# Attention outputs made transposed, with probabilities divided before the product

## The chip, the cores and the metric

The kernel runs on one core of one Trainium2 chip. The metric is the device time of one execution in microseconds (us). A TensorE matmul holds one operand still in the array (the stationary one, loaded by LDWEIGHTS, up to 128 columns) and streams the other through it (the moving one). In the profile PE is the matmul side of TensorE, PEld its weight loads, DVE is VectorE, ACT ScalarE, POOL GpSimd, SP SyncE, which only issues DMAs here.

## What is computed

Eight batches of eight heads attend over 512 local tokens and 32 global ones, with head size 64. Then a mixture of eight experts, with weights from eight rounds of row and column division, runs over all 4352 tokens.

```python
s_g = scale * q_g @ concat(k_g, k_l).T          # 32 global queries see all 544 keys
out_g = softmax(s_g) @ concat(v_g, v_l)
s_ll = where(abs(i - j) <= 32, scale * q_l @ k_l.T, -1e9)
s_lg = scale * q_l @ k_g.T                      # local queries see a band and 32 global keys
out_l = softmax(concat(s_lg, s_ll)) @ concat(v_g, v_l)
x = attention outputs as (tokens, 512)
P = exp(x @ w_gate - max); 8 times: divide rows, divide columns, scale
out = sum over experts e of P[:, e] * (relu(x @ w1[e]) @ w2[e])
```

The experts' first product needs x with its 512 features on partitions: the persistent tile xT.

## The kernel before

**Units.** The attention stage goes through 32 units, one for each batch and head pair (index n, or s for the loop's turn). A unit's 512 queries are cut into eight blocks of 64. Block i sees a band of 128 keys and the 32 global keys, so its scores are 160 columns. The two heads of a pair lie on the two halves of the partitions, so one block is a tile of 128 rows (2 heads x 64 queries).

**Steps of a unit.** st_A transposes q and k on TensorE and spreads them (kTe, qbd). st_B, in three parts of three, three and two blocks, makes scores in PSUM (tile sc), lets VectorE apply the mask and find each row's extreme (ms, mx, L304) and lets ScalarE take the exponential (Pu, L307). st_D1 transposes the band part of the eight blocks on TensorE (ptw, L344) and VectorE copies it out (pw, L346). st_D2 does so for the global part: GpSimd gathers it (Pl, L341), TensorE transposes (L352), ScalarE copies (pg, L354). st_E, for the even blocks (par 0, values va) and the odd ones (par 1, values vb, shifted by 64 keys), multiplies: the transposed probabilities are stationary and V of the pair moves, 130 columns with a column of ones behind each head's 64 values. So the PSUM tile po has queries on its partitions, and the row sums stand in two of its columns. VectorE takes reciprocals (rr, L380) and multiplies them in on the way out (xn, L383). st_X transposes xn on TensorE (L361) and ScalarE copies it into xT (L362).

**Global groups.** Four heads' global queries of one batch form a group; there are 16. st_G0 spreads the queries on GpSimd (qgbd, L396), st_G1 makes 128x544 scores (sg, in po's PSUM buffer), VectorE takes the maximum (L408) and scales it (L409), ScalarE the exponential (Pg, L411). st_G2 transposes Pg in five pieces (L419, copied to pgs by ScalarE, L421). st_G3 multiplies by V (L431, L432) and divides on the way out, in turn on ScalarE (L444) and VectorE (L441), into xgn; st_G4 transposes xgn twice in all (L449, L451).

**Order.** Nothing is moved by a scheduler: each engine executes its instructions in the order in which the program text issues them. One turn s of the main loop runs: st_X(s-2), st_D1(s-1), two f1, st_B(s) part 0, st_D2(s-1), st_G2, st_B part 1, f2, st_E(s-1) par 0, st_A(s+1), f1, st_B part 2, st_E(s-1) par 1, st_G3, f2, logits (every fourth turn), f1 (from turn 9), st_G1, then DMAs and casts. st_G1 runs in turns 4 to 7 and then in every odd turn; st_G2 and st_G3 one turn later. The f1 and f2 are pieces of the experts 0 and 1 that fill TensorE: f1 is four matmuls (ph, L470) with a relu copy to hT on ScalarE or VectorE, f2 eight matmuls (py, L484) with a copy to yst (L487). Turns 0 to 3 have a loop of their own.

**Buffers in PSUM.** ps_mm has two (f1, f2), ps_sc two (scores, global outputs), ps_tr two (all transposes), ps_po one of two banks (po and sg). A buffer is written again only when its last reader is done.

After the stage come the routing weights (lines 842 to 913) and the experts 2 to 7 (lines 921 to 954), which the change does not touch.

Of the kernel before, what the change touches and what calls it, by code (L numbers as in the profile page):

```python
# [23 lines left out]
def kernel(  # L24
# [33 lines left out]
    VW = Dh + 1  # L58
# [30 lines left out]
    with tc.tile_pool(name="att_c", bufs=1) as att_c, \  # L89
# [17 lines left out]
        vgz = [att_c.tile([P, 4, H, VW], FP16, name=f"vgz{i}") for i in range(2)]  # L107
        qgbd = [att_c.tile([P, 2, P], FP16, name=f"qgbd{i}") for i in range(2)]
        vab = [(att_c.tile([P, NJ, H, VW], FP16, name=f"va{i}"),
                att_c.tile([P, NJ, H, VW], FP16, name=f"vb{i}")) for i in range(2)]  # L110
        xgn = [att_c.tile([P, D], FP16, name=f"xgn{i}") for i in range(2)]
# [35 lines left out]
        def select_v(b, t, js, both=True):  # L147
            for j in js:
                c0 = P * j + HB * t
                pv = ps_mm.tile([P, D], FP32, tag="mm", name="pv")  # L150
                for so in range(NJ):
                    nc.tensor.matmul(pv, zsel[:, so, c0 : c0 + P], vsr[:, so], start=(so == 0), stop=(so == NJ - 1))
                cp = nc.vector.tensor_copy if both and j % 2 == 0 else nc.scalar.copy
                cp(out=vab[b % 2][t][:, j, :, 0:Dh], in_=pv.rearrange("p (h d) -> p h d", h=H))
# [4 lines left out]
        def load_vz(b):  # L159
            for i in range(4):  # L160
                nc.sync.dma_start(out=vgz[b % 2][W * i : W * (i + 1), i, :, 0:Dh], in_=vg16[b])
# [7 lines left out]
        def load_v(b):  # L169
            va, vb = vab[b % 2]  # L170
            vz = vgz[b % 2]
            src = v_l[b].rearrange("h s d -> s h d")

            def first():
                load_vg(b)
                nc.gpsimd.dma_start(out=va[W:P, 0, :, 0:Dh], in_=src[0:96])

            def mid(j):
                nc.gpsimd.dma_start(out=va[:, j, :, 0:Dh], in_=src[P * j - W : P * j + 96])

            def last():
                nc.gpsimd.dma_start(out=vb[HB : HB + W, NJ - 1, :, 0:Dh], in_=src[Sl - W : Sl])
                move_vb(b)
                load_vz(b)

            return [first] + [lambda j=j: mid(j) for j in range(1, NJ)] + [last]
# [25 lines left out]
        def init_vgz(t, eng):  # L212
            eng.memset(t, 0.0)
            for i in range(4):
                eng.memset(t[W * i : W * (i + 1), i, :, Dh:VW], 1.0)

# [23 lines left out]
        for va, vb in vab:  # L240
            nc.vector.memset(va[:, :, :, Dh:VW], 1.0)
            nc.vector.memset(vb[:, :, :, Dh:VW], 1.0)
# [41 lines left out]
        def st_B(n, part):  # L284
            b, hp = divmod(n, HP)
            qb, kt = qbd[n % 2], kTe[n % NK]
            if part == 0:
                st[n] = dict(Pu=att_wk.tile([P, NHB, SW], FP16, tag="Pu", name="Pu"),
                             mx=att_wk.tile([P, NHB], FP32, tag="mx", name="mx"))
            d = st[n]  # L290
            i0 = 3 * part
            ni = min(3, NHB - i0)
            sc = ps_sc.tile([P, 512], FP32, tag="sc")
            ms = att_wk.tile([P, 3, SW], FP32, tag="ms")
            for ii in range(ni):
                i = i0 + ii
                nc.tensor.matmul(sc[:, SW * ii : SW * ii + KW], qb[:, i, :],  # L297
                                 kt[:, HB * i : HB * i + KW], start=True, stop=True)
                nc.tensor.matmul(sc[:, SW * ii + KW : SW * (ii + 1)], qb[:, i, :],  # L299
                                 kgT[:, hp, Sg * b : Sg * (b + 1)], start=True, stop=True)  # L300
            for ii in range(ni):
                i = i0 + ii
                mi = 0 if i == 0 else (2 if i == NHB - 1 else 1)
                nc.vector.tensor_tensor_reduce(  # L304
                    out=ms[:, ii, :], in0=sc[:, SW * ii : SW * (ii + 1)], in1=mask[:, mi, :],
                    scale=-scale, scalar=BIG, op0=ALU.add, op1=ALU.min, accum_out=d["mx"][:, i : i + 1])
                nc.scalar.activation(out=d["Pu"][:, i, :], in_=ms[:, ii, :], func=AF.Exp, scale=-1.0,  # L307
                                     bias=d["mx"][:, i : i + 1])

        def st_B0(n, part):  # L310
            b, hp = divmod(n, HP)
            qb, kt = qbd[n % 2], kTe[n % NK]
            if part == 0:
                st[n] = dict(Pu=att_wk.tile([P, NHB, SW], FP16, tag="Pu", name="Pu"),
                             mx=att_wk.tile([P, NHB], FP32, tag="mx", name="mx"))
# [17 lines left out]
            for ii in range(ni):  # L333
                i = i0 + ii
                nc.scalar.activation(out=d["Pu"][:, i, :], in_=sc[:, SW * ii : SW * (ii + 1)], func=AF.Exp,
                                     scale=-1.0, bias=d["mx"][:, i : i + 1])

        def st_D1(n):
            d = st[n]
            d["Pl"] = att_wk.tile([P, NHB, Sg], FP16, tag="Pl", name="Pl")  # L340
            nc.gpsimd.tensor_copy(out=d["Pl"], in_=d["Pu"][:, :, KW:SW])  # L341
# [14 lines left out]
        def st_X(n):  # L356
            b, hp = divmod(n, HP)
            xn = st.pop(n)["xn"]
            pt = ps_tr.tile([P, NJ, P], FP16, tag="tr")
            for j in range(NJ):  # L360
                nc.tensor.transpose(pt[:, j, :], xn[:, j, :], identity)  # L361
            nc.scalar.copy(out=xT[:, hp, Sl * b : Sl * (b + 1)], in_=pt.rearrange("p j q -> p (j q)"))  # L362

        def st_E(n, par):
            b, hp = divmod(n, HP)
            d = st[n]
            va, vb = vab[b % 2]
            vz = vgz[b % 2]
            if par == 0:
                d["xn"] = att_wk.tile([P, NJ, P], FP16, tag="xn", name="xn")  # L370
            vx = va if par == 0 else vb
            po = ps_po.tile([P, NJ, 256], FP32, tag="po")
            for j in range(NJ):
                i = 2 * j + par
                nc.tensor.matmul(po[:, j, 0 : 2 * VW], d["pw"][:, i, :], vx[:, j, 2 * hp : 2 * hp + 2, :],  # L375
                                 start=True, stop=False)
                nc.tensor.matmul(po[:, j, 0 : 2 * VW], d["pg"][:, i // 4, :], vz[:, i % 4, 2 * hp : 2 * hp + 2, :],  # L377
                                 start=False, stop=True)
            rr = att_wk.tile([P, NJ], FP32, tag="rr")
            nc.vector.reciprocal(out=rr, in_=po[:, :, Dh])  # L380
            for a in range(2):
                r = slice(HB * a, HB * (a + 1))
                nc.vector.tensor_tensor(out=d["xn"][HB * par : HB * (par + 1), :, Dh * a : Dh * (a + 1)],  # L383
                                        in0=po[r, :, VW * a : VW * a + Dh],
                                        in1=rr[r].unsqueeze(2).to_broadcast([HB, NJ, Dh]), op=ALU.mult)
# [12 lines left out]
        def st_G1(b, g):  # L398
# [8 lines left out]
            m2 = att_wk.tile([P, 2], FP32, tag="m2")  # L407
# [3 lines left out]
            nc.scalar.activation(out=Pg, in_=sg[:, 0:S], func=AF.Exp, scale=scale, bias=m2[:, 1:2])  # L411
            gs[(b, g)] = Pg

        def st_G2(b, g):
            Pg = gs[(b, g)]
# [8 lines left out]
        def st_G3(b, g):  # L424
# [3 lines left out]
            po = ps_sc.tile([P, 512], FP32, tag="sc")  # L428
            hs = slice(4 * g, 4 * g + 4)
            for t in range(NJ):  # L430
                nc.tensor.matmul(po[:, 0 : 4 * VW], pgs[:, t, :], vb[:, t, hs, :], start=(t == 0), stop=False)  # L431
            nc.tensor.matmul(po[:, 0 : 4 * VW], pgs[:, 4, :], vz[:, 3, hs, :], start=False, stop=True)  # L432
            rg = att_wk.tile([P, 1], FP32, tag="rg")
            nc.vector.reciprocal(out=rg, in_=po[:, Dh : Dh + 1])
            xg = xgn[b // 4]
            o = slice(W * (b % 4), W * (b % 4 + 1))
            for hh in range(4):
                r = slice(W * hh, W * (hh + 1))
                h = 4 * g + hh
                if hh % 2:  # L440
                    nc.vector.tensor_scalar(out=xg[o, Dh * h : Dh * (h + 1)], in0=po[r, VW * hh : VW * hh + Dh],  # L441
                                            scalar1=rg[r, 0:1], scalar2=None, op0=ALU.mult)
                else:
                    nc.scalar.mul(xg[o, Dh * h : Dh * (h + 1)], po[r, VW * hh : VW * hh + Dh], rg[r, 0:1])  # L444

        def st_G4(hf):
            pt = ps_tr.tile([P, HP, P], FP16, tag="tr")
            for dk in range(DP):
                nc.tensor.transpose(pt[:, dk, :], xgn[hf][:, P * dk : P * (dk + 1)], identity)  # L449
            t0 = (GT0 + hf) * P  # L450
            nc.scalar.copy(out=xT[:, :, t0 : t0 + P], in_=pt)  # L451
# [99 lines left out]
        for s in range(HP):  # L551
# [5 lines left out]
            if s >= 2:  # L557
                st_X(s - 2)
# [24 lines left out]
            st_A(s + 1)  # L583
            if s == 1:
# [16 lines left out]
        for s in range(HP, NU + 2):  # L601
# [8 lines left out]
            if s == HP:  # L610
                st_D1(s - 1)
                st_D2(s - 1)
                st_X(s - 2)
# [4 lines left out]
                st_X(s - 1)  # L618
# [8 lines left out]
            else:  # L627
                if s > HP + 1:
                    st_X(s - 2)
                if s > NU:  # L630
                    break
# [11 lines left out]
            if s < NU:  # L643
                st_B(s, 1)
            f2("a")
# [5 lines left out]
            if s < NU:  # L651
                st_B(s, 2)
            if s > HP:
# [9 lines left out]
            if s == 17:  # L663
                st_G4(0)
            if s == NU:
                st_G4(1)
# [319 lines left out]
```

## Time and profile before

| | us |
|---|---|
| three runs: lowest, median, highest | 1085.76, 1086.7, 1090.41 |
| the profiled execution: its time | 1088.94 |
| its span, first to last instruction | 1087.2 |
| attention stage, last copy into xT ends | about 359 |

Busy times inside the attention stage, of 50 us from 200 to 250: PE 49.44, DVE 35.44, ACT 37.09, POOL 13.43. The granted TensorE clock is 1.00 there and 0.991 over the span.

| group | engine | count | mean ns |
|---|---|---|---|
| L307 exponential, 128x160 | ACT | 224 | 422 |
| L304 mask and extreme, 128x160, and its read of the result | DVE | 224 | 321 and 83 |
| L380 reciprocal 128x4 | DVE | 64 | 180 |
| L383 division on the way out, 64x256 | DVE | 128 | 422 |
| L361 transposes of outputs | PE | 128 | 221 |
| L362 copy into xT, 128x512 | ACT | 32 | 585 |
| L341 gather Pl, 128x256 | POOL | 32 | 400 |
| L129 casts of q and k, 128x1024 | POOL | 30 | 1046 |

Matmuls are pipelined: one row lasts longer than the step to the next. So TensorE's cost is read from the starts of neighbours, not from the mean. A line of the timeline gives start, length, engine, line, operation and, in brackets, how long the engine had stood idle before it and what ended that.

### The profile page before, as it was taken

To read this page: it belongs to the slowest core of one execution; us is meant where nothing else is said; L and a number is where in the kernel's file an instruction comes from. 1 tells how busy PE (TensorE), PEld (TensorE's weight loads), DVE (VectorE), ACT (ScalarE), POOL (GpSimd) and SP (SyncE) were. 2 spreads that over 40 slices of the span, in tenths; PEclk is the share of its full clock that TensorE was granted. 3 is DMA by queue.
4 is the path that set the end of the run, shared out by engine and by line. 5 is a ranking of instruction groups with operands and counts; after the bars stand their busy time and mean duration, and the time that the engine had idled before them with its cause. 6 is when DMAs were issued, how large, how long until landed. Compare 5 with 4: busy or idle time off the path is not lost.

```text
span 1087.2 us, 19737 instructions
## 1 busy us (share of the span) xinstructions
PE 1050.2 (97%) x7988; PEld 685.3 (63%) x7988; DVE 697.7 (64%) x1504; ACT 540.2 (50%) x1091; POOL 126.6 (12%) x232
## 2 busy tenths in 40 slices
PE   7689999999999999999999999999999999999987
PEld 4555665666665455666666666666666666666676
DVE  6667676767676666768457466576575474485474
ACT  5658777777766445334334334343343343343332
POOL 7251332231401500000000000000000000000000
PEclk8989999999999999999999999999999999999999
DMA  9956676785753977423423424524424334234242
GB/s 257 195 99 168 101 170 184 114 181 145 136 103 66 215 172 289 184 97 137 174 98 136 175 97 141 185 87 175 179 99 173 137 136 175 97 136 144 104 169 79
DMA packets 102963, 160.55 MB, mean 148 GB/s; under 512 B 40909, under 2 KB 75865, under 8 KB 91865
## 3 DMA queue, kind: packets, MB, share of 16 engines
q1 hardware_dynamic: 52376, 120.03, 32.4%
q0 software_dynamic: 46736, 20.20, 15.3%
q10 hardware_dynamic: 3760, 19.08, 4.5%
q8 instruction: 62, 1.02, 0.4%
q14 instruction: 29, 0.23, 0.1%
HBM read 149.24 MB, written 33.40 MB: 168 GB/s over the span
## 4 chain that ended last, share of the span: by engine, by line
PE 81%; DVE 9%; DMA 3%; ACT 2%; issue 2%; SPq 1%; POOL 0%; DVEq 0%; ACTq 0%; POOLq 0%
PE ph L772 32%; PE m L808 20%; PE pm L808 8%; PE ph L470 8%; PE py L484 7%; DVE xn L383 3%; DMA qgf<-in_q_g_dram 1%; DVE hT L475 1%; PE sc L297 1%; PE po L377 1%; DVE ms L304 1%; PE po L375 1%; DMA pb<-pd 1%; SPq L192 1%; ACT yst L487 1%
## 5 line engine op out<-in xcount | busy, mean ns | idle before, releaser
L774 ACT ACTIVATE h<-ph 128x512 f16<-128x512 f32 (+1 forms) x432 | 247.1, 573 | 397.7 <-PE ph L772 393.8
L772 PE MATMUL ph<-xs,w1s 128*128 128x512 f16 (+1 forms) x1728 | 405.3, 367 | 3.6 <-DMA w1s<-w1d 2.3
L772 PEld LDWEIGHTS <-w1s 128*128 128x128 f16 x1728 | 169.0, 98 | 128.3 <-issue 2.6
L814 DVE SCALAR_TENSOR_TENSOR o<-pm,o 128x512 f32<-128x512 f32 (+1 forms) x106 | 70.6, 667 | 241.3 <-PE pm L808 241.0
L808 PEld LDWEIGHTS <-h 128*128 128x128 f16 x1616 | 158.1, 98 | 48.4
L808 PE MATMUL m<-w2c,s 128*128 128x256 f16 x1212 | 158.3, 273 | 0.0
L808 PEld LDWEIGHTS <-s 128*128 128x128 f16 x1212 | 118.6, 98 | 43.8
L470 PE MATMUL ph<-xT,w1e 128*128 128x512 f16 (+1 forms) x576 | 135.2, 368 | 3.7 <-DVE lg L459 1.4
L484 PE MATMUL py<-w2e,hT 128*128 128x512 f16 x544 | 128.3, 379 | 0.1
L708 DVE TENSOR_TENSOR xs<-xT,pb 128x2048 f16<-128x2048 f16 (+2 forms) x57 | 117.2, 2060 | 11.1 <-DMA pb<-pd 11.1
L808 PE MATMUL m<-w2c,h 128*128 128x256 f16 x808 | 105.5, 273 | 0.0
L808 PE MATMUL pm<-w2c,h 128*128 128x256 f16 x808 | 96.9, 273 | 0.0
L708 DVE TENSOR_TENSOR s<-h 128x2048 f16<-128x2048 f16 (+1 forms) x106 | 92.3, 912 | 4.5 <-ACT h L774 4.5
L470 PEld LDWEIGHTS <-w1e 128*128 128x128 f16 x576 | 54.6, 99 | 51.5 <-issue 6.8
L484 PEld LDWEIGHTS <-hT 128*128 128x128 f16 x544 | 50.8, 97 | 51.0 <-issue 0.2
L307 ACT ACTIVATE Pu<-ms,mx 128x160 f16<-128x160 f32 x224 | 80.8, 422 | 3.2 <-DVE mx L304 1.7
L304 DVE CUSTOM_DVE_ANT_0 ms<-sc,mask 128x160 f32<-128x160 f32 x224 | 59.7, 321 | 34.6 <-PE sc L299 17.9
L708 DVE TENSOR_TENSOR h<-h 128x1024 f16<-128x1024 f16 (+1 forms) x106 | 65.6, 660 | 0.0
L383 DVE TENSOR_TENSOR xn<-po,rr 64x256 f16<-64x256 f32 x128 | 54.0, 422 | 3.1
L473 ACT ACTIVATE hT<-ph 128x512 f16<-128x512 f32 (+1 forms) x91 | 48.9, 564 | 13.8 <-PE ph L470 11.4
L814 DVE SCALAR_TENSOR_TENSOR o<-m,o 128x512 f32<-128x512 f32 (+1 forms) x90 | 52.2, 653 | 0.4
L487 ACT COPY yst<-py 128x512 f32<-128x512 f32 x68 | 39.5, 581 | 21.0 <-PE py L484 18.7
(156 smaller groups left out, 971.1 us busy)
## 6 DMA issues: line engine op xcount, KB each, us to landing
w1s<-w1d SPq DMA_DIRECT2D x54, 1024.0 KB
yd<-yst ACTq DMA_DIRECT2D x16, 1024.0 KB
pb<-pd SPq DMA_DIRECT2D x48, 256.0 KB
o<-yd SPq DMA_DIRECT2D x8, 1024.0 KB
y<-yd SPq DMA_DIRECT2D x8, 1024.0 KB
out_dram<-o SPq DMA_DIRECT2D x8, 1024.0 KB
f<-in_q_l_dram SPq DMA_DIRECT2D x15, 512.0 KB
f<-in_k_l_dram SPq DMA_DIRECT2D x15, 512.0 KB
```

Source lines behind the costliest of these rows:

```text
L304: nc.vector.tensor_tensor_reduce(out=ms[:, ii, :], in0=sc[:, SW * ii : SW * (ii + 1)], in1=mask[:, mi, :], scale=-scale, scalar=BIG, op0=A ...
L307: nc.scalar.activation(out=d["Pu"][:, i, :], in_=ms[:, ii, :], func=AF.Exp, scale=-1.0, bias=d["mx"][:, i : i + 1])
L383: nc.vector.tensor_tensor(out=d["xn"][HB * par : HB * (par + 1), :, Dh * a : Dh * (a + 1)], in0=po[r, :, VW * a : VW * a + Dh], in1=rr[r]. ...
L470: nc.tensor.matmul(ph[:, 0:n], wts[e][0][:, dk, P * fm : P * (fm + 1)], xT[:, dk, c0 : c0 + n], start=(dk == 0), stop=(dk == DP - 1))
L473: nc.scalar.activation(out=hT[:, fm, 0:n], in_=ph[:, 0:n], func=AF.Relu)
L484: nc.tensor.matmul(py, hT[:, fk, P * c : P * (c + 1)], wts[e][1][:, fk, :], start=(fk == 0), stop=(fk == FT - 1))
L487: nc.scalar.copy(out=ys[:, c, :], in_=py)
L708: nc.vector.tensor_tensor(out=out, in0=in0, in1=in1, op=op)
L772: nc.tensor.matmul(ph[:, 0:n], w1s[i][:, dk, P * fm : P * (fm + 1)], xss[i][:, dk, 0:n], start=(dk == 0), stop=(dk == DP - 1))
L774: nc.scalar.activation(out=hs[i][:, fm, 0:n], in_=ph[:, 0:n], func=AF.Relu)
L808: nc.tensor.matmul(pm[:, HD * t : HD * (t + 1)], lhs[0][:, k, lhs[1] + P * t : lhs[1] + P * (t + 1)], w[:, q - 1, k, :], start=(k == 0 and ...
L814: nc.vector.scalar_tensor_tensor(out=o, in0=pm[:, 0 : HD * nt].rearrange("p (t d) -> p t d", d=HD), scalar=sg / float(E), in1=o, op0=ALU.m ...
```

## The change

V of the pair becomes the stationary operand and the transposed probabilities move. The product then comes out with the pair's 128 features on partitions and 64 queries of each head side by side, as xT wants it; of each 128x128 block the two 64x64 diagonal parts are used. The sums come from the exponentials themselves (accum_out), and a new step st_N divides the probabilities before they are transposed: a reciprocal for each part and a multiply for each block on VectorE, and one multiply with a broadcast for the global part on GpSimd, which now makes Pl. st_X and st_G4 go, with the ones columns (130 columns become 128, and vgz lands in rows of 1024 bytes instead of 128). For global groups st_GN divides Pg, ahead of st_D1 in the text.

```diff
-                                     bias=d["mx"][:, i : i + 1])
+                                     bias=d["mx"][:, i : i + 1], accum_out=d["sm"][:, i : i + 1])
...
+        def st_N(n, part):
...
+            nc.vector.reciprocal(out=d["rs"][:, i0:i1], in_=d["sm"][:, i0:i1])
+            for i in range(i0, i1):
+                nc.vector.tensor_scalar(out=d["Pu"][:, i, 0:KW], in0=d["Pu"][:, i, 0:KW], scalar1=d["rs"][:, i : i + 1],
+                                        scalar2=None, op0=ALU.mult)
+            if part == 2:
...
+                nc.gpsimd.tensor_tensor(out=d["Pl"], in0=d["Pu"][:, :, KW:SW],
+                                        in1=d["rs"].unsqueeze(2).to_broadcast([P, NHB, Sg]), op=ALU.mult)
...
-            d["Pl"] = att_wk.tile([P, NHB, Sg], FP16, tag="Pl", name="Pl")
-            nc.gpsimd.tensor_copy(out=d["Pl"], in_=d["Pu"][:, :, KW:SW])
...
+                nc.tensor.matmul(po[:, i, :], vx[:, j, 2 * hp : 2 * hp + 2, :], d["pw"][:, i, :], start=True, stop=False)
+                nc.tensor.matmul(po[:, i, :], vz[:, i % 4, 2 * hp : 2 * hp + 2, :], d["pg"][:, i // 4, :],
                                  start=False, stop=True)
...
+            if par == 1:
+                for a, cp in ((0, nc.scalar.copy), (1, nc.vector.tensor_copy)):
+                    r = slice(HB * a, HB * (a + 1))
+                    cp(out=xT[r, hp, Sl * b : Sl * (b + 1)].rearrange("p (i q) -> p i q", q=HB), in_=po[r, :, r])
...
+        def st_GN(b, g):
+            Pg, m2 = gs[(b, g)]
+            nc.vector.reciprocal(out=m2[:, 3:4], in_=m2[:, 2:3])
+            nc.vector.tensor_scalar(out=Pg, in0=Pg, scalar1=m2[:, 3:4], scalar2=None, op0=ALU.mult)
...
+            for pr in range(2):
+                hs = slice(4 * g + 2 * pr, 4 * g + 2 * pr + 2)
+                qs = slice(HB * pr, HB * (pr + 1))
+                for t in range(NJ):
+                    nc.tensor.matmul(po[:, pr, :], vb[:, t, hs, :], pgs[:, t, qs], start=(t == 0), stop=False)
+                nc.tensor.matmul(po[:, pr, :], vz[:, 3, hs, :], pgs[:, 4, qs], start=False, stop=True)
...
+                cp(out=xT[r, 2 * g : 2 * g + 2, t0 : t0 + Sg], in_=po[r, :, Sg * a : Sg * (a + 1)])
```

The calls in a turn of the main loop:

```diff
             else:
-                if s > HP + 1:
-                    st_X(s - 2)
-                if s > NU:
-                    break
+                if g23:
+                    st_GN(*gp)
                 st_D1(s - 1)
...
                 st_B(s, 1)
+                st_N(s, 0)
...
                 st_B(s, 2)
+                st_N(s, 1)
             if s > HP:
                 st_E(s - 1, 1)
...
             f2("a")
-            if s == 17:
-                st_G4(0)
-            if s == NU:
-                st_G4(1)
+            if s < NU:
+                st_N(s, 2)
```

In turns 0 to 3 the three parts of st_N stand together behind st_A(s+1).

## Prediction

> **What bounds the kernel now.** I read the page's busy times first, then its slices, then a table of stretches, the chain of waits, and the timelines of single engines over two units.
>
> ```profile
> PE 1050.2 (97%) x7988; PEld 685.3 (63%) x7988; DVE 697.7 (64%) x1504; ACT 540.2 (50%) x1091; POOL 126.6 (12%) x232
> ```
>
> TensorE is busy nearly all the time. The change touches the attention stage alone, which ends near 359 us, so that stage is what counts:
>
> ```profile
> core 0: us, PE busy (x) PEld busy (x) DVE busy (x) ACT busy (x) POOL busy (x), PEclk, DMA share, GB/s
> 200.00:250.00 50.00, 49.44 (x463) 31.00 (x461) 35.44 (x140) 37.09 (x87) 13.43 (x25) 1.00 0.66 134
> ```
>
> In a stretch of 50 us TensorE idles 0.56. VectorE works 71% of it and ScalarE 74%: both have room on the average. What counts is whether each of their results is there when TensorE, which takes its instructions in order, comes to need it. The chain of waits gives the period of two units (a unit is one head pair; every second one carries a global group):
>
> ```profile
> 198.18 1.73 PE ph L470 x8
> ...
> 219.20 1.73 PE ph L470 x8
> ```
>
> So a pair of units lasts 21.02 us. TensorE's own steps, added from the starts in its timeline, make 20.64; 0.38 is waiting.
>
> Now ScalarE over one unit that carries a global group:
>
> ```profile
> 219.67 0.71 ACT L411 ACTIVATE Pg<-sg,m 128x544 f16<-128x544 f32 x1 [1.74 <-DVE m L409]
> 220.28 0.57 ACT L362 COPY xT<-pt 128x512 f16<-128x512 f16 x1
> 220.75 1.10 ACT L473 ACTIVATE hT<-ph 128x512 f16<-128x512 f32 x2
> 221.74 1.07 ACT L307 ACTIVATE Pu<-ms,mx 128x160 f16<-128x160 f32 x3
> 222.71 0.35 ACT L354 COPY pg<-pt 128x256 f16<-128x256 f16 x1
> 222.96 0.69 ACT L421 COPY pgs<-pt 128x640 f16<-128x640 f16 x1
> 223.55 1.07 ACT L307 ACTIVATE Pu<-ms,mx 128x160 f16<-128x160 f32 x3
> 224.51 0.57 ACT L487 COPY yst<-py 128x512 f32<-128x512 f32 x1
> 225.85 1.17 ACT L282 COPY qbd<-pt 64x512 f16<-64x512 f16 x2 [0.77 <-DVE kTe L273]
> 227.05 0.75 ACT L307 ACTIVATE Pu<-ms,mx 128x160 f16<-128x160 f32 x2
> ```
>
> The reader is to see that from 219.67 to 227.80 it stands still once, for 0.77 us. And two engines that read one score tile take turns, though their partitions differ:
>
> ```profile
> 207.23 0.30 ACT L444 ACTIVATE xgn<-po,rg 32x64 f16<-32x64 f32 x1 [0.45 <-DVE rg L434]
> 207.57 0.28 DVE L441 TENSOR_SCALAR xgn<-po,rg 32x64 f16<-32x64 f32 x1 [0.37 <-ACT xgn L444]
> ```
>
> **The change part by part.** TensorE first. Four transposes of outputs go from each unit: four of L361 take 0.22 us in a row (starts 0.055 apart). The global product goes from five matmuls of 260 columns (0.54 us, starts 0.11 apart) to ten of 64. No row has 64 columns with a new weight: the 32-column score matmuls and the 8-column logits matmuls both step by 0.027 us, the 128-column ones by 0.055. I take 0.027, thus 0.27 us (at 0.055 nothing is won). The pair product goes from 130 to 128 columns, 0.8 ns each. A pair of units saves 2 x 0.22 + 0.27 + 32 x 0.0008 = 0.74 us. The two groups of L449 go as well (0.44 us in all).
>
> ScalarE: the exponentials give sums. Whether this costs an instruction the trace does not show. VectorE's counterpart does: DVE_READ_ACCUMULATOR2, 83 ns, 224 times. Ends: nothing, and 202 ns (L244, an ACTIVATE of one column). I take 0.083, the same job on the neighbour; eight a unit make 0.66 us. The copy L362 (0.585) is replaced by a copy of 64x512 (0.58, as L282).
>
> VectorE: per unit two L380 and four L383 go, 2.05 us. Three reciprocals (0.18, as L380), eight divides of 128x128 and one copy of 64x512 (0.69, as L154) come. A divide between SBUF tiles of f16 has no row. Ends: 0.154 (L409, one column) and 0.287 (L848, 128x128 to f32); I take 0.21, as the f16 copy L548 of that shape. Sum 0.54 + 1.68 + 0.69 = 2.91. Each global group loses 0.74 (L434, two L441) and gains a reciprocal 0.17, a divide of 128x544 (ends 0.154 and 0.72, one column and one element a cycle; taken 0.44, at L346's pace) and a copy 0.22. VectorE goes from 7.4 to about 8.3 us per unit of 10.5, ScalarE from 7.8 to about 8.3. Neither is full. The loss is in the order:
>
> A. The divide of the global probabilities (st_GN) stands on VectorE ahead of the copy pw, and the global transposes on TensorE need both: Pg divided, and the PSUM buffer that pw frees. Count from the end of the global scores (218.37). In the profile the exponential ends at 220.38, 2.01 later. Add the sum's read 0.08, reciprocal 0.17, divide 0.44, pw 0.68 and four hand-overs of 0.04 (rr to xn): 3.54. TensorE is there after ptw 0.45, two ph 1.73, scores 0.24 and two transposes 0.11: 2.53. It waits 1.0; with VectorE later by 0.4 from the unit before (step C), 1.4. Before, pw ran while the exponential did.
>
> B. The unit's last divides (part 2) stand on VectorE behind its copy of the outputs, which waits for ScalarE's copy of the same tile (the turn-taking above), which stands behind the last exponentials. First exponential at 3.54 + 0.4 + 0.37 (L304's 0.32 and a hand-over) = 4.3. ScalarE then needs 2.77 (221.74 to 224.51), yst 0.57, qbd 1.17, exponentials 0.75, eight reads 0.66, copy 0.58: done at 10.8. Then VectorE's copy 0.69, the global copy 0.22, reciprocal 0.18, two divides 0.42, hand-overs 0.16: 12.5. TensorE, late by A, comes to the seventh probability transpose of the next unit at 2.53 + 1.4 + 7.46 + 0.33 = 11.7 (7.46 are its steps from the global transposes on). It waits 0.8. Before, these transposes needed only exponentials, long done.
>
> C. In the other unit the same queue holds the copies of the outputs until 10.5; the next global scores need that buffer and come at 10.3: 0.1 to 0.2, and VectorE's backlog pushes A by 0.4. The copy pg also slips behind its first matmul: 0.1.
>
> New waits 1.4 + 0.8 + 0.1 + 0.1 = 2.4 a pair; saved work 0.74; of the old waits some 0.3 (L470 behind yst L487 and behind lg L459) go under the new ones. Net +1.35 a pair. Units 9 to 32 make 12 pairs: +16.2. In units 5 to 8 each carries a group and there is one f1 less before the scores: waits of about 1.9, less 0.49 of work and 0.5 of old waits, +0.9 each: +3.6. At the start TensorE idles until q_g has landed (53.5 us); the change saves nothing there, and Pl, now behind the divides, holds back GpSimd's casts and the loads on SP's queue behind them by up to 1.1 us, with the DMA engines full anyway: +0.5. vgz lands in longer rows (32 KB each as now), behind q_g in its queue: nothing. At the end the two last output transposes with their waits (0.62 and 0.24) go: -1. Sum +19.3. The profiled execution took 1088.94 (span 1087.2), so it would take 1108.2; on the median, 1086.7 + 19.3 = 1106.0.
>
> A rule against the waits in B: the Trainium skill, PSUM — Partial Sum Buffer, section on bank collisions, has two engines collide only in the same bank and quadrant, so the halves of po could be copied side by side. The trace differs in what is done: all 32 of L441 wait for ScalarE. Were the rule used, B and C would shrink by 0.69 us and the sum by some 8 us.
>
> **Rivals.** 1. TensorE stays the bound and the change is faster. Place: the global transposes (A) and the seventh transpose (B). It holds if the new waits of a pair stay under 0.74 + 0.3 = 1.04 us. For it: VectorE and ScalarE are only 71 and 74% busy, and TensorE loses real work. Against it: A alone is 1.0 with no delay from elsewhere. With no wait at all: 12 x -1.04, 4 x -0.5, -1: -15.5, 1071 us. Chance 0.10.
>
> 2. The costs taken are at their low ends: the sum comes free, the divide of Pg takes 0.15. Then B falls to 0.14, C to nothing, A to about 1.1: +0.2 a pair, with start, end and units 5 to 8 about +3 in all: 1090. For it: ScalarE has free time in the other units. Chance 0.16.
>
> 3. The divides wait for GpSimd. They are the first VectorE operations of the stage that both read and write SBUF alone, and GpSimd is busy 13.43 of 50 us with casts of 1.046. If the two exclude each other, each of some 3.5 groups of divides a unit meets a busy GpSimd with chance 0.27 and waits half a cast: 0.47 a unit, over 28 units +13 on the forecast: 1119; with the sum's read at its high end of 0.2 (B and C each 0.9 more) up to 1145. The trace of before has no such pair of operations in this stage. The Trainium skill, SBUF — State Buffer, Who interferes with whom, states this exclusion for tensor_scalar in its two-port modes; no run here shows it yet. Chance 0.14.
>
> **How the numbers follow.** The forecast of 1106 has 0.60, with its own range of 1092 to 1128. The bounds of the read (0 to 0.2) and of the divides carry it from 1087 to 1145; the range that leaves out most of rival 1 and the far end of rival 3 is 1084 to 1138. Under about 0.5% (5.4 us) this kernel's measurement does not tell a change from none. Faster by more: rival 1, 0.10. Within: rival 2 with a little of the forecast's edge, 0.16. Slower: 0.74.
>
> **What would show it.** Right: L419's successor waits for DVE pw, over 0.8 us each; the ptw transposes wait for VectorE's divide; VectorE's xT copy waits for ScalarE's; TensorE in 200 to 250 us falls from 49.44 to about 44.5 busy; the pair of units lasts 22.4 us. Wrong: TensorE still near 49 there (rival 1); no row for reading sums on ScalarE (rival 2); divides whose times scatter by up to a cast (rival 3). It goes wrong above all if the read costs far from 0.083, as eight stand in each chain.

## The result, and the profile after

The changed kernel takes 1118.3 us (median of four runs, 1117.4 to 1122.7) against 1086.2 for the kernel before in the same session (1084.7 to 1090.4): ratio 1.030, 95% interval 1.026 to 1.034, so it is slower by 32 us. The profiled execution has a span of 1120.9 us and took 1122.7, the longest of the four; the other three lie at 1117.4 to 1118.8. Most of that difference seems to lie in its first 60 us, as will be seen.

First the page's busy times and the stretch from 200 to 250 us, the same views as of before:

```profile
PE 1053.5 (94%) x7932; PEld 679.6 (61%) x7932; DVE 734.7 (66%) x1692; ACT 555.2 (50%) x1345; POOL 132.6 (12%) x224
```

```profile
200.00:250.00 50.00, 44.63 (x412) 26.96 (x413) 37.73 (x157) 36.24 (x115) 13.25 (x23) 1.00 0.64 139
```

TensorE's busy time in that stretch falls from 49.44 to 44.63 us, at the full granted clock both times, while VectorE is 75% and ScalarE 72% busy. No engine is full over the stretch, so the time goes into waits between them. The chain of waits of the changed kernel shows the hand-overs (start, duration, what ran):

```profile
210.24 1.73 PE ph L459 x8
...
217.27 0.93 ACT Pu L301 x4
218.23 0.59 ACT xT L380
218.84 0.69 DVE xT L380
219.57 0.18 DVE rs L339
219.77 0.80 DVE Pu L341 x2
...
221.39 0.64 DVE m L404
...
222.30 0.81 ACT Pg L407 x2
...
223.34 0.36 DVE Pg L414
223.70 0.60 DVE pw L354
...
224.63 1.34 ACT Pu L301 x6
...
226.82 1.25 ACT Pu L301 x6
...
233.41 1.74 PE ph L459 x8
```

This pair of units lasts 23.17 us; the same pair took 22.00 before (186.84 to 208.84). Pairs differ in length: the one of 21.02 us that the prediction shows lasts 22.69 now, and the mean of the ten pairs from unit 10 to unit 30 (counted from 0) goes from 21.45 to 23.12. From 217.27 to 233.19 us TensorE is not in the chain at all. First come the last exponentials with their sums (4 entries: two exponentials, two reads), ScalarE's copy of the outputs, VectorE's copy of the same tile, the reciprocal, the last divides and the maximum of the next global scores. Then the global exponential on ScalarE at 222.30, the divide of the global probabilities, and only then the copy pw that sets TensorE free. From there ScalarE runs on through the next unit's exponentials and reads, the copies pgs, yst and qbd, and its own copy of the outputs up to 231.17. Before the change the divides were not in this row, pw did not stand behind one, and a row of three exponentials took 1.07.

What TensorE waits for, between 60 and 370 us (total us, times, longest), with VectorE's wait for ScalarE's copy:

```profile
DVE xT L380 <- ACT xT L380: 20.1, 26, 1.3
PE pt L421 <- DVE pw L354: 13.7, 13, 1.3
PE ptw L352 <- DVE Pu L341: 9.0, 22, 2.4
PE sg L402 <- DVE xT L380: 4.8, 8, 2.1
```

These are the places A, B and C of the prediction, in this order of size. To see where the time collects, I compare the moment of the last probability transpose of some units in the two traces (units counted from 0; the prediction counts them from 1):

| up to | later than before by, us | the prediction's steps |
|---|---|---|
| unit 4 | 9.3 | start +0.5 |
| unit 8 | 15.0 (5.7 more) | units 5 to 8, +3.6 |
| unit 31 | 34.4 (19.3 more) | pairs, +16.2 |
| end of span | 33.8 (0.6 less) | end -1 |

### The profile page after: what moved, and what is told of

Read it like the earlier page. It is cut to its first block, busy times and chain, and to the rows that moved or that the text cites. A ratio compares the mean times of both kernels' runs of the same rounds, so it can differ in the third digit from the quotient of the medians.

```text
span 1120.9 us, 20061 instructions
## 1 busy us (share of the span) xinstructions
PE 1053.5 (94%) x7932; PEld 679.6 (61%) x7932; DVE 734.7 (66%) x1692; ACT 555.2 (50%) x1345; POOL 132.6 (12%) x224
## 4 chain that ended last, share of the span: by engine, by line
PE 67%; ACT 13%; DVE 11%; DMA 1%; issue 1%; ACTq 0%; POOL 0%; DVEq 0%
PE ph L757 31%; PE m L793 19%; PE pm L793 8%; ACT Pu L301 6%; PE ph L459 4%; PE py L473 3%; ACT qbd L275 3%; DVE Pu L341 2%; DVE xT L380 2%; ACT xT L380 1%; ACT Pg L407 1%; DVE hT L464 1%; DVE m L404 1%; ACT pgs L423 1%; DMA pb<-pd 1%
## 5 line engine op out<-in xcount | busy, mean ns | idle before, releaser
L301 ACT ACTIVATE Pu<-ms,mx 128x160 f16<-128x160 f32 x224 | 93.6, 420 | 9.9 <-DVE mx L298 8.2
L341 DVE TENSOR_SCALAR Pu<-Pu,rs 128x128 f16<-128x128 f16 x256 | 69.4, 337 | 3.4
```

The lines of the kernel that those rows point to most:

```text
L341: nc.vector.tensor_scalar(out=d["Pu"][:, i, 0:KW], in0=d["Pu"][:, i, 0:KW], scalar1=d["rs"][:, i : i + 1], scalar2=None, op0=ALU.mult)
```

## The experiments

Theory: TensorE waits at several places because new work stands in VectorE's queue ahead of what TensorE needs (A, B, C), and a similar order spoils the start. Main rival: ScalarE, which now reads out eight sums a unit, is simply the bound. Second rival (rival 3 of the prediction): GpSimd holds VectorE's divides. All runs side by side, against runs of the kernel before on the same chip; "won" is the difference of its ratio to 1.0297 times 1086.2 us; the two last columns come from the traces, as in the table above (how much later than before at unit 10, and the loss per pair of units from unit 10 to 30):

| run | ratio (95%) | won, us | unit 10, us | per pair, us |
|---|---|---|---|---|
| the change | 1.0297 (1.0257 to 1.0337) | - | +18.1 | +1.67 |
| e1_split_start | 1.0243 (1.0224 to 1.0262) | 5.9 | +13.8 | +1.67 |
| e2_pl_copy | 1.0180 (1.0160 to 1.0199) | 12.7 | +10.8 | +1.16 |
| e3_gn_behind_pw | 1.0201 (1.0172 to 1.0229) | 10.4 | +12.1 | +1.07 |
| e4_vector_first | 1.0269 (1.0241 to 1.0297) | 3.0 | +12.4 | +1.66 |
| e11_vector_first_both | 1.0183 (1.0164 to 1.0202) | 12.4 | +14.2 | +0.82 |
| e6_divides_first | 1.0159 (1.0134 to 1.0185) | 15.0 | +12.6 | +0.39 |
| e5_no_reads | 1.0143 (1.0111 to 1.0175) | 16.7 | +12.8 | +0.89 |
| e8_before_reads | 1.0023 (1.0001 to 1.0045) | - | -2.6 | +0.16 |
| e7_four | 0.9994 (0.9979 to 1.0009) | 32.9 | +6.3 | -0.28 |
| e10_four_no_reads | 0.9905 (0.9890 to 0.9920) | 42.6 | -1.8 | -0.56 |
| e9_four_fill | 0.9981 (0.9970 to 0.9992) | 34.3 | +6.5 | -0.29 |
| e12_four_casts_early | 0.9999 (0.9985 to 1.0013) | 32.4 | +4.4 | -0.34 |

Every figure in the column "won" is counted from the change's own ratio, whose interval is 4.3 us either way, and that is common to all of them. The kernel before had medians of 1089.7 to 1090.6 us beside the experiments and 1086.2 beside the change, so the column may be too large by some 4 us throughout; the gains of e1_split_start and e4_vector_first are not clear of that. Runs are better told apart by the last column.

The column "unit 10" scatters with the start: e3_gn_behind_pw and e6_divides_first have the same turns 0 to 3 as the change, but at unit 3 they stand at +5.2 and +5.3 us, the change at +9.8. That is about the 4.4 us by which the change's profiled execution lies over its median, so a usual start loses some 4.5 us less than the profile shows (an estimate). The last column repeats within 0.01 where an edit does not touch the stage (e1 against the change).

**The start.**

```
             st_A(s + 1)
+            if s < 2: select_v(0, s, range(2))
             for part in range(3): st_N(s, part)
-            (select_v of all four blocks behind it)
+            (select_v of the last two blocks behind it)
```

> Edit: in turns 0 and 1 the divides stand between the second and the third copy of selected V on VectorE, not ahead of the first. Theory (VectorE's order costs the start): in the changed kernel the first probability transposes of units 0 and 1 begin at 20.9 and 32.0 us of the span, against 17.8 and 26.1 before the change; here near 18.5 and 27.5, the wait of 2.8 us for VectorE's va goes, and 3 to 6 us are won: 1112 to 1115, from 1118. Rival (GpSimd's casts and memsets hold the divides wherever they stand): the third copy then waits instead, under 2 us are won, and divides of turn 0 still take 1 us or more.

5.9 us were won by the ratios, with intervals that just overlap. In the trace unit 1's transposes come 0.2 us later than before, against 5.8 in the change and 2.1 and 2.2 in e3 and e6, which have the change's first turns; the loss per pair is unchanged, as it must be. So VectorE's queue did cost the start: in the changed kernel the copies of selected V, which TensorE needs for the next V block, stand behind the divides. TensorE waits 2.8 us for one of these copies. VectorE's timeline of the change in turn 0:

```profile
12.60 1.44 DVE L341 TENSOR_SCALAR Pu<-Pu,rs 128x128 f16<-128x128 f16 x3
...
15.66 3.52 DVE L341 TENSOR_SCALAR Pu<-Pu,rs 128x128 f16<-128x128 f16 x2
```

Three divides take 1.44 us here, two 3.52; three in the steady units take 0.58:

```profile
217.51 0.58 DVE L341 TENSOR_SCALAR Pu<-Pu,rs 128x128 f16<-128x128 f16 x3
...
219.77 0.80 DVE L341 TENSOR_SCALAR Pu<-Pu,rs 128x128 f16<-128x128 f16 x2
```

GpSimd's timeline has the rest: at 12.63 and 14.31 us casts of 1.04 us, at 15.29 the issue of a load (0.78), at 16.09 the product Pl (0.63), at 16.65 another issue (0.63), at 17.27 a memset of 1.82. The slow divides end within 0.1 us of the two casts and of the memset.

**GpSimd's product Pl.** The product needs only exponentials and reciprocals, so in each unit it starts together with the last two divides: hence 0.80 us for two, where 0.42 would do.

```
-                nc.vector.tensor_scalar(out=Pu[:, i, 0:KW], in0=Pu[:, i, 0:KW], ...)
+                nc.vector.tensor_scalar(out=Pu[:, i, :], in0=Pu[:, i, :], ...)
-            (Pl = Pu * rs on GpSimd in st_N, part 2)
+            (Pl = copy of Pu on GpSimd at the head of st_D1, as before the change)
```

> Edit: the divide takes all 160 columns of a block, and Pl is again a plain copy on GpSimd, which has to wait for the divides. Theory (GpSimd's product Pl, which starts as soon as the reciprocals are there, holds one of the last two divides): the pair of last divides falls from 0.80 to about 0.43 us, no divide of the steady units is over 0.30 us, the transposes' waits for VectorE's divides (9.0 us between 60 and 370 us) fall under 3, and 5 to 11 us are won: 1107 to 1113. Rival (divides are slow for another reason, and ScalarE's chain is the bound): divides stay at a mean of 0.33 us, the time stays within 3 us of 1118.

12.7 us were won, a little over the range. Some 6 of them are in the steady pairs (0.51 a pair); the rest lies ahead of unit 10, where Pl stood beside the divides too. The groups of the divides in that run (busy us, mean ns, idle before):

```profile
L341 DVE TENSOR_SCALAR Pu<-Pu,rs 128x160 f16<-128x160 f16 x256 | 53.9, 263 | 5.5
L412 DVE TENSOR_SCALAR Pg<-Pg,m 128x544 f16<-128x544 f16 x16 | 9.7, 609 | 0.6
```

The mean divide falls from 337 to 263 ns, though it is 25% longer; in the changed kernel the 169 divides with no GpSimd operation beside them have a mean of 251 ns, the other 87 of 505. But the divide of the global probabilities rises from 370 to 609 ns. Six of the 16 take 0.75 to 1.09 us, the undisturbed ones 0.36: the first ends behind a cast of GpSimd's, the other five 0.13 to 0.22 us behind GpSimd's issue of a load of V (0.89 us), which had begun just ahead of them. One collision was cured, another, cheaper one was made. The probability transposes' waits fell to 5.4 us only, not under 3. The rival that divides are slow for another reason falls.

**The global divide (A).**

```
-                if g23: st_GN(*gp)
                 st_D1(s - 1)
+                if g23: st_GN(*gp)
```

> Edit: the divide of the global probabilities stands on VectorE behind the copy pw, not ahead of it. Theory (step A of the prediction): pw runs while ScalarE makes the global exponential, the global transposes come 0.6 us earlier in each of 16 groups, their wait (15.4 us in the whole run, for pw) falls under 7 and is now for the divided Pg, and 6 to 11 us are won: 1107 to 1112. Rival (ScalarE with its eight sum reads a unit is the bound): the transposes' wait falls, but it comes back as waits for ScalarE's copies and exponentials; under 3 us won.

10.4 us, at the top of the range. Waits between 60 and 370 us in that run:

```profile
PE ptw L352 <- DVE Pu L341: 9.5, 24, 2.4
PE pt L421 <- DVE Pg L414: 5.7, 11, 0.7
```

The global transposes wait 5.7 us where they waited 13.7, now for the divide itself; B is untouched. The loss per pair falls by 0.60 us. A is shown.

**The copies of the outputs (B).** First the order of the two engines on the output tile:

```
-                for a, cp in ((0, nc.scalar.copy), (1, nc.vector.tensor_copy)):
+                for a, cp in ((1, nc.vector.tensor_copy), (0, nc.scalar.copy)):
```

> Edit: VectorE takes its half of the output tile first, ScalarE second. Theory (step B: the last divides stand behind a copy that waits for ScalarE's copy of the same tile): VectorE's waits for ScalarE's copy (29 us in the run) go, its divides come 0.6 us and more earlier, the probability transposes' waits (9.0 us) fall under 3 and the global transposes' waits shrink with them; 8 to 18 us are won: 1100 to 1110. Rival (ScalarE is the bound): its copy now waits for VectorE's, up to 0.3 us a unit; the time stays within 4 us of 1118, or is longer.

The theory missed: 3.0 us, within the rival's 4 and not clear of nothing won; the loss per pair is unchanged at 1.66. VectorE's timeline shows why:

```profile
224.64 0.69 DVE L380 CAST xT<-po 64x512 f16<-64x512 f32 x1
226.09 0.23 DVE L440 CAST xT<-pog 64x64 f16<-64x64 f32 x1 [0.75 <-ACT xT L440]
```

The copy of the outputs waits no more, but the small copy of the global outputs behind it does: ScalarE goes first on that tile, and comes late, since it now waits for VectorE on the other. The divides behind both are no earlier. So the same swap in both tiles:

```
-            for a, cp in ((0, nc.scalar.copy), (1, nc.vector.tensor_copy)):   # also in st_G3
+            for a, cp in ((1, nc.vector.tensor_copy), (0, nc.scalar.copy)):
```

> Edit of the changed kernel: VectorE takes its half first of both tiles, outputs and global outputs (the run before swapped the outputs alone and found VectorE waiting for ScalarE's copy of the global outputs, 11.3 us in all). Theory (that second wait is why nothing was won): VectorE's waits for ScalarE's copies are gone, the probability transposes' waits fall under 6 us, and 5 to 12 us are won: ratio 1.019 to 1.025. Rival (the divides wait for the sums of the last exponentials, not for the copies; the swap moves nothing on the path): ratio 1.026 to 1.030.

12.4 us, just past the range, and the transposes' waits for a divide fall from 9.0 to 0.3: the second wait was the reason. The other cure puts the divides ahead of the copies:

```
                 st_N(s, 1)
+                st_N(s, 2)
...
-            if s < NU: st_N(s, 2)      # was behind st_E, st_G3 and f2
```

> Edit: the last two divides of a unit stand on VectorE ahead of its copies of the outputs. Theory (step B, and the copies' wait for ScalarE): VectorE spends that wait on the divides, the probability transposes no longer wait for a divide (from 9.0 to under 2 us), the next maximum of the global scores starts 0.5 us earlier, and 8 to 16 us are won: ratio 1.015 to 1.022. Rival (as in the run with VectorE's half first, where a wait only moved): the wait comes back for the global scores behind the copies of the outputs, over 10 us in all, and under 4 us are won.

```profile
PE sg L402 <- DVE xT L380: 8.8, 9, 2.5
...
PE ptw L352 <- DVE Pu L341: 0.3, 1, 0.3
```

15.0 us. The transposes' wait is gone; the global scores, which need the tile that the copies free, wait 8.8 us where they waited 4.8: part of what the rival said, and less than what is won. The loss per pair falls to 0.39 us, the lowest of any single edit.

**The sums.** If it is the order alone, taking the sums' reads away should bring less than that:

```
-                nc.scalar.activation(..., bias=mx, accum_out=sm)      # sm -> a constant 1 for the reciprocal
+                nc.scalar.activation(..., bias=mx)
```

> Edit: the exponentials give no sums; reciprocals and divides stay, but work on a constant 1, so the outputs are left undivided. Theory (waits come from VectorE's order; ScalarE's reads of 0.09 us only lengthen the way to the last divides): the read's rows go, three exponentials take 1.07 us again, the probability transposes' waits shrink, and 4 to 10 us are won: ratio to before 1.020 to 1.026, from 1.0297. Rival (ScalarE's eight reads a unit are the bound): 0.74 us a unit come back, 15 to 21 us are won: ratio 1.010 to 1.016.

16.7 us: the theory's band is missed and the rival's is hit. Without sums the reciprocals need not wait for them either, so this prices the reads together with that wait. Yet the reads by themselves cost little, as the kernel before with the same eight reads a unit shows:

> Edit of the kernel before the change: its exponentials also write their sums, to a tile that nothing reads. Theory (in the order of before ScalarE's reads lie in its idle time and behind work that TensorE does not need soon): ratio 0.999 to 1.005. Rival (eight reads a unit are a price wherever the divide stands): 0.5 us and more a unit, ratio 1.012 or more.

2.5 us (0.1 to 4.9), 0.16 a pair. So the reads have no fixed price, and neither VectorE's order alone nor ScalarE's work alone is the bound: the chain above runs through both, one behind the other. In the order of before TensorE waits for no exponential between 60 and 350 us; in that of the change the divides come behind the last ones, and eight reads of up to 0.09 us lengthen ScalarE's row by up to 0.7 us a unit. Shortening it (e5) or taking the divides out from behind the copies (e6) brings some 15 us, either way.

**All four edits.** e1, e2, e3 and e6 together:

> Edit: the split start, Pl as a copy with divides of 160 columns, the global divide behind pw, and the last divides ahead of the output copies, all four together. Theory (the places add up, as each is a wait of its own on TensorE): the single gains of 5.9, 12.7 and 10.4 us and that of the last edit sum to some 35 us, and TensorE's saved work shows: ratio 0.992 to 1.003. Rival (they are one chain through VectorE and ScalarE, so that the second cure finds the wait already gone): ratio 1.008 to 1.015.

Ratio 0.9994: no difference from before that can be measured. The single gains sum to 44.0 us and the four bring 32.9, but the sum holds the uncertainty of the change's ratio four times, so these two do not show an overlap. The pairs do: singly the four edits take 0, 0.51, 0.60 and 1.28 us off a pair, 2.39 in all, and together 1.95. The waits overlap by a fifth there: neither one chain nor quite separate. TensorE from 200 to 250 us:

```profile
200.00:250.00 50.00, 47.92 (x456) 28.95 (x455) 39.74 (x164) 37.55 (x119) 18.05 (x30) 1.00 0.76 147
```

TensorE is busy for 47.92 us of the 50, with less work a pair; between 60 and 370 us its largest wait is the global scores' for VectorE's copy of the outputs, 5.6 us. From unit 10 on each pair is 0.28 us shorter than before: here the saved matmuls show at last. What uses this up is the 6.3 us lost up to there. Without the reads:

> Edit: the kernel with the four edits, its exponentials without sums, reciprocals and divides on a constant 1, so the outputs are left undivided. Theory (the reads cost 16 us in the changed kernel because the last divides, and through VectorE the global scores, hang on the end of ScalarE's row of exponentials; with the four edits that chain has slack): at most 5 us are won, ratio 0.995 to 1.000. Rival (0.74 us of ScalarE a unit is a price in any order): ratio 0.980 to 0.988.

9.7 us between the two, outside both bands. It is ahead of e7_four by 1.7 us at unit 3, 4.3 at unit 4, 6.4 at unit 8, 8.1 at unit 10 and 10.9 at unit 30. So with the four edits the reads cost 0.28 us a pair in the steady pairs, and most of their price lies ahead of them: in the turns where every unit carries a global group, as far as the scatter of the start lets this be told. This part of the theory (slack everywhere) falls.

**Two trials to go below.** Keeping TensorE busy at the start of e7_four, and moving GpSimd's casts in it:

```
+            if s >= 2:
+                for i in range(10): nc.tensor.matmul(idle, identity, kTe[s][:, 0:Sl], start=True, stop=True)
```

> Edit: the kernel with the four edits, and at the end of turns 2 and 3 ten matmuls of 512 columns more, whose product nothing reads, where TensorE would stand (3 us before unit 2). Theory (idle TensorE of the start is followed by stretches at half the granted clock, 27 us of them before 66 us against 10 in the kernel before, and these cost): the half-clock records before 66 us fall to 14 us or less, and 2 to 5 us are won: ratio 0.995 to 0.998, from 0.9994. Rival (at the start TensorE waits for data anyway, a full clock only makes it wait longer): ratio 0.999 to 1.003.

Inconclusive: 0.9981 against 0.9994 for e7_four, intervals that overlap, though against the kernel before it is some 0.2% shorter. The expectation had one figure wrong: the kernel before has 17 us at half clock before 66 us, not 10. The fill brought e7_four's 27 us to 20, and units 4 to 31 of both profiles stand within 0.4 us of each other, so in the profile the clock of the start was worth nothing; that execution took 1090.49 us, the longest of its twelve.

```
-                    vq = load_v(b + 1); run(vq[:3]); cast_qk(b + 1, 1, gq)
+                    cast_qk(b + 1, 1, gq); vq = load_v(b + 1); run(vq[:3])
```

> Edit of the kernel with the four edits: GpSimd casts the second half of q and k ahead of issuing the loads of V, no longer behind them. In that kernel six of the 16 divides of the global probabilities stand beside these casts and take 0.75 to 0.80 us, the other ten 0.36. Theory (a GpSimd operation on SBUF holds a divide on VectorE until it ends): the six fall to 0.36, TensorE's waits for the divided Pg (2.5 us) fall under 1, and 1 to 3 us are won: ratio 0.996 to 0.9985, from 0.9994. Rival (a divide of 0.75 us delays nothing that TensorE needs by then, or the casts now hold the last divides of the unit instead): ratio 0.999 to 1.002.

The rival: 0.9999. The waits for the divided Pg fall from 2.5 to 1.8 us only. Only one of the 16 divides of the global probabilities stands beside a cast now (0.79 us), but five take 0.62, and beside each of these GpSimd issues loads of V (0.89 us an issue). The collision moved again, to the one that e2 had shown.

## Why the prediction was right, and where it was not

The direction and the mechanism held, the size fell short: 1106 was forecast, in a range of 1092 to 1128 for the forecast alone, and 1118 came. In the profiled execution 33.8 us were lost where the sum had 19.3; of these 14.5 us, 8.8 lie in the start, 2.1 in units 5 to 8, 3.1 in the pairs and 0.4 at the end.

- **TensorE's saved work.** 0.74 us a pair taken. Over the ten pairs from unit 10 to 30 its rows are busy for 21.17 us a pair before, 21.02 after and 20.62 in e7_four. The 0.55 of e7_four is the nearest to the saving, as few waits are left there; in the changed kernel rows reach into the waits, since a row lasts longer than the step to the next (0.22 against 0.055 us for a transpose). The 64-column matmuls step by 0.029 us (ten from 111.33 to 111.62), 0.027 taken. The prediction found no row of 64 columns with a new weight, but the trace of before has some: eight transposes (L201) from 31.717 to 31.917 us, 0.029 apart.
- **The reads.** They are there, as rows of their own (busy us, mean ns); three exponentials with theirs start to end in 1.25 to 1.34 us, against 1.07 before, so 0.06 to 0.09 each; 0.083 taken. That half of the loss hangs on them, the prediction's last warning, e5 showed (16.7 of 32 us).

```profile
L301 ACT ACTIVATE Pu<-ms,mx 128x160 f16<-128x160 f32 x224 | 93.6, 420 | 9.9 <-DVE mx L298 8.2
L301 ACT ACTIVATION_READ_ACCUMULATOR Pu<-ms,mx 128x1 f32 x224 | 42.3, 189 | 0.0
```

- **The divides.** 0.21 taken; in a row they step by 0.165, so three take 0.58, less than taken. The last two take 0.80, not 0.42: Pl on GpSimd, which the sum left out. The divide of Pg takes 0.36; 0.44 taken. VectorE is busy for 8.66 us a unit (8.3 forecast), ScalarE for 8.26 (8.3).
- **A, B, C.** From 200 to 340 us the global transposes wait 8.1 us in seven groups, 1.16 each (1.4 taken); the probability transposes 3.8 us in six pairs, 0.63 (0.8 taken); the global scores and ph 1.9 us, 0.3 a pair (0.2 taken). TensorE's idle time a pair rises from 0.28 to 2.10 over the ten pairs, by 1.82; the sum had 2.4 less 0.3. The forecast of 44.5 us busy met 44.63 in its stretch, but the ten pairs make 45.5 of 50: so close a hit was luck.
- **The pairs.** 1.35 net taken, 1.67 measured; from unit 8 to 31, 11.5 pairs, that is 19.3 us, where the sum had 16.2 for 12. The pair of 21.02 us became one of 22.69, where 22.4 was forecast. Part of this closeness is luck: e2 shows that 0.51 of the 1.67 hang on Pl beside the divides, which the sum did not have, so without that the pair's loss (1.16) would have come out under the 1.35.
- **Units 5 to 8** lose 5.7 us, where 3.6 was taken.
- **The start is the term that failed.** "At the start TensorE idles until q_g has landed (53.5 us); the change saves nothing there", +0.5 in all. It lost 9.3 us in the profiled execution, an estimated 4 to 5 in a usual one (that execution lies 4.4 us over the median; e3, with the same turns, stands at 4.0). I had counted what lies behind Pl in GpSimd's queue and on SP's, but not the copies of selected V behind the divides in VectorE's, nor the casts beside these divides. TensorE does not only wait for q_g there: it makes V first, and wants VectorE for it.
- **Rival 3** was real, mostly at other places than the casts: its price was sized by half a cast at random (0.47 us a unit), and the collision comes from the unit's own Pl, by design, in every unit. For the rule of the Trainium skill on this (SBUF — State Buffer, "Who interferes with whom": the first to issue holds the shared port pair for its whole instruction, and tensor_scalar in a two-port mode wants it) the trace agrees: a divide of 0.25 us took 1.12 beside a cast of 1.04. The prediction says that the trace of before has no such pair in the stage. It has such a pair just ahead of turn 0: VectorE's copy of k from SBUF to SBUF (L539, 128x512) took 2.22 us beside GpSimd's memset of 1.91 and 0.93 beside a cast of 1.04, and in the changed kernel, where it began ahead of the cast, 0.40. With these rows rival 3 deserved more than 0.14.
- **The rule of the Trainium skill on PSUM** (PSUM — Partial Sum Buffer, bank collisions) was set aside rightly: 31 of VectorE's 32 copies of the outputs wait for ScalarE's, 29.4 us in all. These are waits of the program; whether the chip would need them no run shows.

## What to carry to other kernels

Dividing ahead of a product and not behind it moves the divide from the end of a unit's work, where TensorE hardly waited for it (3.1 us between 60 and 350), into the row exponentials, sums, divide, transposes; then what stands on two engines' queues between the last exponential and the divide delays TensorE. The sums' reads, 1.0 to 1.4 us of ScalarE's time a pair, cost 0.78 a pair here and 0.16 in the old order. Before such a move, write down for each queue what stands between the two ends, on every stage and the start above all, and place the divide first; here three edits of the order and one of Pl together were worth as much as the whole loss (ratio 1.0297 to 0.9994). A GpSimd operation whose inputs become ready together with a VectorE divide on SBUF will stand beside it in every round, as Pl did here: make one wait for the other, and look where its neighbours on GpSimd then fall.

## What the runs showed of the hardware

- A divide from SBUF to SBUF on VectorE that begins about when a GpSimd operation on SBUF does, or during it, ends only when that ends: 0.25 us alone, 0.63 beside Pl, 1.12 beside a cast, over 3 beside Pl, a memset and two issues of loads in a row. One that begins 0.13 us ahead of Pl still takes 0.26. Issues of loads by GpSimd alone held the divide of 128x544 too: five of those in e12 took 0.62 us and five in e2 0.99 to 1.09, against 0.36. Not every issue does: in e12 the divides at 74.42 and 350.00 us took 0.36 beside one.
- Reading out ScalarE's sum shows as 189 ns, but delays the next exponential by some 0.09 us at most.
- The granted clock halves after little work, not after none. The change spends 34 us at half clock ahead of its end in seven stretches of 3.4 or 6.8 us, the kernel before 17 in three. In the 3.4 us ahead of each stretch of these two and of e7_four TensorE was busy 13 to 63% of the time, as its matmul rows add up (before: 30, 39 and 25%; the change: 38, 30, 13, 63, 30, 37 and 40%; e7_four: 48, 33, 61, 22 and 53%). The Trainium skill (TensorE: Matmul & The Clock Gate, "What's actually happening") has the clock fall after an idle window of 3.4 us; the length agrees, but here every window of up to 40% at full clock was followed by half, and of those between 41 and 63% some, so it need not be idle. Half the clock can cost at most half of the 17 us more; how much it did is open.
